# Chunked attention and two mixture-of-experts layers on one core: another order for the attention's loads

## The chip, the cores and the metric

The kernel runs on one core of a Trainium2 chip. A core has TensorE (PE, matrix multiplication; PEld is its weight load), VectorE (DVE), ScalarE (ACT), GpSimd (POOL) and SyncE (SP), each with an instruction stream of its own that is worked off in order, and 16 DMA engines that move data for all of them. Nearly every transfer of this kernel is issued by SP; GpSimd issues the gathers, the scatters and a few copies.

The metric is the device time of one execution in microseconds (us). A profiled execution gives a trace with the start and length of every instruction. Rows of the trace count from the start of its span.

## The reference

Attention runs over `q`, `k`, `v` of shape (2, 8, 768, 64): two batches, eight heads, 768 positions, head size 64. Its output, 1536 rows of 512 numbers, goes through a layer of eight experts with the two best per row, and that layer's output through a second layer of eight experts with one per row and a capacity of 384.

```python
for c in range(768 // 32):                       # chunks of 32 queries
    q_c   = q[:, :, 32*c:32*c+32]
    k_ctx = k[:, :, max(0, 32*c-16):min(768, 32*c+40)]
    k_full = concat([mem_k, k_ctx]);  v_full = concat([mem_v, v_ctx])
    s = (q_c @ k_full.T) / 8
    a = exp(s - max(s));  a = a / (sum(a) + 1e-9)
    out[:, :, 32*c:32*c+32] = a @ v_full
x = out as (1536, 512)
x = sum over each row's two best experts of gate * (relu(x @ w1[e]) @ w2[e])
y = gate * (relu(x @ v1[e]) @ v2[e])             # one expert, if a place is free
```

Every chunk sees the eight memory rows `mem_k`, `mem_v` beside its own context.

## The kernel before

**Attention.** The 1536 rows are 12 tiles of 128, numbered t = 0 to 11; 0 to 5 belong to the first batch, 6 to 11 to the second. A loop runs `step(t)` for t = -2 to 11 as a pipeline: step t makes the scores of tile t + 2 (L240) and their maxima and differences (L253, L256), the transposed probabilities of tile t + 1 (L267, L269), attends with the values of tile t (L281), turns tile t - 1 for its gate logits (L306, L309) and makes those of tile t - 2 (L316), and at its end divides tile t by its sums (`normalise`, L290 to L297). Keys and queries come into SBUF as raw blocks (L120, six per batch, 512 KB each) and are turned on TensorE (`t_unit`, L207) into `kt` and `qz`. The first batch's are turned ahead of the loop. The second batch's turns are 13 units (one of them the memory keys, L197) in a list, from which each step takes as many as the tuple `UP` says: the first half ahead of the probabilities, the second half behind the attending.

Values are loaded per tile and per batch in two shifted copies (L128, 24 loads, rows of 256 bytes). The memory rows are written over certain partitions of each copy from a small tile (`v_mem`, L136), so a `v_mem` waits for its loads, and `L281` for the `v_mem`. The first batch's `v_mem` is issued by POOL, the second's by SP.

**What sets the order.** The schedule is written out by hand: each engine works its instructions in the order of the program. The dictionary `ahead` lists what is issued ahead of which step; -3 stands for ahead of the loop. SP therefore issues all loads of the attention first, and the result of tile t, `put_x(t)` (L300, 256 KB to `x_rows` in memory), can be issued only when SP has come to it, at the start of step t + 1. The result tiles `xs` have four buffers, so `normalise(t)` may write only when `put_x(t - 4)` has landed. The accumulators `psC` of L281 hold one tile, so `attend(t + 1)` waits for `normalise(t)`.

**Behind the attention.** From step 7 on `half_step`, called twice in a step, also splits the first experts' weights (`raww`, L726) into a high and a low part, `whi` on ACT (L743) and `wlo` on DVE (L744); `SPS` says how many at each call. The list of expert jobs follows: V0 and V8 for the first layer's expert 0, S[0] to S[6] for the rest, then U0, UL and R[0] to R[6] for the second layer. Hooks attach other work to the units of a job: eight zero fills of the second layer's input rows (`blank_rows`, L1237, 520 KB each) hang on V0 and V8. A job's `pool` names those of every four splits of the next weights whose low part GpSimd makes instead of DVE.

Of the kernel before, what the change touches and what calls it, by code (L numbers as in the profile page):

```python
# [25 lines left out]
AT = {2: ('lg',), 4: ('w',), 5: ('gw',), 18: ('w',), 24: ('rank',), 27: ('list',), 29: ('w',), 30: ('w',), 32: ('end',)}  # L26
NS = 0
QUICK = 0.7
UP = (0, 3, 3, 3, 3, 1)
WPR = 1  # L30
UU = [0, 0, 0.5, 1, 1, 1.5, 1.5, 1.5, 2, 2, 3, 3]
UWE = 3
# [6 lines left out]
CP = 0.8  # L39
CPP = 2.4  # L40
AH = (0.5, 0.0)
SPS = [2, 0, 3, 0, 1, 1, 2, 1, 2]
RB = 6
ZB = 2
ZT = 5
# [9 lines left out]
def attention_two_moe_kernel(  # L55
# [7 lines left out]
    nc = tc.nc  # L63
# [5 lines left out]
    G = S // 128  # L69
# [19 lines left out]
    def pool(name, side="left", **kw):  # L89
        st_ = ExitStack()  # L90
        pools[name] = st_
        return st_.enter_context(tc.tile_pool(name=name, bufs=1, side=side, **kw))
# [31 lines left out]
    def load_v(b, g, y):  # L124

        r = 128 * g + 32 * y - 16
        p0, p1 = max(0, -r), min(128, S - r)
        nc.sync.dma_start(vw[b][y][p0:p1, g, :, 0:D],  # L128
                          bass.AP(tensor=v.tensor, offset=v.offset + (b * H * S + r + p0) * D,
                                  ap=[[D, p1 - p0], [S * D, H], [1, D]]))  # L130

    def v_mem(b, g0, g1, eng):

        for y in range(2):
            for x in range(2):
                eng.dma_start(vw[b][y][64 * x + 56:64 * x + 64, g0:g1].rearrange("p g h d -> p g (h d)"),  # L136
                              memv[:, b].rearrange("p h d -> p (h d)")[:, None].to_broadcast([NM, g1 - g0, H * (D + 1)]))
# [161 lines left out]
    def put_x(t):  # L299
        nc.sync.dma_start(x_d[NP + 128 * t:NP + 128 * t + 128, 0:DM], xs(t))  # L300
# [22 lines left out]
    def step(t, units):  # L323

        on = 0 <= t < NT
        end = t == NT - 1
        n = UP[t + 2] if t + 2 < len(UP) else 0

        def some(m):
            for _ in range(m):  # L330
                if units:
                    units.pop(0)()

        if t + 2 < NT:
            scores(t + 2)
            submax(t + 2)
        half_step()
        if end:
            flush()
            low = x_block(V0.xg[0], 0, V0.C, "B", True)  # L340
        some((n + 1) // 2)
        pe_part()
        if 0 <= t + 1 < NT:
            prob(t + 1)
        if on:
            attend(t)
        some(n // 2)
        if 0 <= t - 1:
            x_tr(t - 1)
        if 0 <= t - 2:  # L350
            logits(t - 2)
        pe_part()
        if end:
            put = logits(NT - 2, True)
            normalise(t)
            low()
            V0.weight(0)
            put()
        elif on:
            half_step()  # L360
            normalise(t)
# [3 lines left out]
    def y_consts():  # L365

        for i in range(2):
            nc.vector.tensor_copy(yid[:, :, i, 0:128], ident[:, None, :].to_broadcast([128, KD, 128]))
            nc.vector.tensor_copy(yid[:, :, i, 128:136], wg2)
        nc.vector.tensor_tensor(yid[:, :, 0, 136:144], wg2, yid[:, :, 0, 128:136], op=OP.subtract)  # L370
        nc.vector.tensor_copy(yid[:, :, 1, 136:144], zero[:, 0:32].rearrange("p (k e) -> p k e", k=KD))
# [861 lines left out]
    raw_q = [(n, j) for n in range(4) for j in range(2)]  # L1233
    split_q, sps = [], list(SPS)

    def blank_rows(z, n, w):
        nc.sync.dma_start(z, zero[:, None, 0:w].to_broadcast([128, n, w]))  # L1237

    def raw_w0():
        n, j = raw_q.pop(0)  # L1240
        half(n, j, w1a, w2a, 0, n)
# [22 lines left out]
    V0 = Job("T", 0, caps1[0], True, cols=0)  # L1264
    V8 = Job("W", 0, caps1[E], True, cols=E)
# [14 lines left out]
    raw1 = []  # L1280
# [25 lines left out]
    def gates2():  # L1306
# [2 lines left out]
        nc.gpsimd.tensor_copy(noi[:, :, E:V], noi[:, :, 0:1])  # L1309

    lv = lambda b, g: [lambda y=y: load_v(b, g, y) for y in range(2)]
    ahead = {-3: [*lv(0, 0), *lv(0, 1), gates, *sum((lv(0, g) for g in range(2, G)), []), *raw1,
                  *[lambda g=g: v_mem(0, g, g + 1, nc.gpsimd) for g in range(2)],
                  *[lambda g=g: v_mem(0, g, g + 2, nc.gpsimd) for g in (2, 4)],
                  gates2, *sum((lv(1, g) for g in range(G)), [])],
             0: [lambda: v_mem(1, 0, 1, nc.sync), lambda: v_mem(1, 1, G, nc.sync)]}
    for f in ahead.pop(-3):
        f()
    zr = x2_d.rearrange("(t p) c -> p t c", p=128)
# [1 line left out]
    zeros = [(zr[:, ZN * i:ZN * i + ZN], ZN, W2) for i in range((N + NP) // (128 * ZN))]  # L1321
    zeros2 = [(zo[:, 4 * i:4 * i + 4], 4, DM) for i in range(N // 512)]
    for t in range(-2, NT):
        if 0 <= t - 1:
            put_x(t - 1)
        for f in ahead.pop(t, ()):
            f()
        if t == ZT:
            blank_rows(x_d[0:NP].rearrange("(t p) c -> p t c", p=128), 4, W1)
        if t == G:  # L1330
            assert not units and not ahead
            pools["a0p"].close()
            wp["A"] = pool("wpA")
            st["x"] = (wp["A"].tile([128, KD, CM], F32R, name="xh"), wp["A"].tile([128, KD, CM], F32R, name="xl"))
            wp["Z"] = pool("wpZ")
            for _ in range(ZB + RWB):
                raw_w0()
            y_consts()
        if t == G + 1:
            split_q = [(n, c) for n in range(3) for c in range(4)]  # L1340
        step(t, units)
        for i, (t0, t1) in enumerate(BT):
            if t - 2 == t1 - 1 and i < len(BT) - 1:
                routes[i] = route(i)
                state["gen"].append(routes[i])
# [19 lines left out]
    UL = Job("T", n2, caps2[E], False, gate=U0.gate)  # L1365
    R = [Job(kind2(caps2[1 + s]), n2 + 4 + 4 * i, caps2[1 + s], False, gate=U0.gate) for i, s in enumerate(ORDER2)]
# [262 lines left out]
    def hook(job, u, f):  # L1629
        hooks.setdefault((at[job], u), []).append(f)  # L1630

    for j, job in enumerate(jobs[:-1]):
        if jobs[j + 1] in S[1:] + R[1:]:
            early_ = job in R and job.kind == "T" and jobs[j - 1].kind == "M"
            hook(*(jobs[j - 1], FU) if early_ else (job, 0), jobs[j + 1].fetch)
    for j in range(len(zeros)):
        hook(*((V0, j) if j < 3 else (V8, j - 2)), lambda j=j: blank_rows(*zeros[(j + 2) % len(zeros)]))
    for j in range(3):
        hook(S[j], 4, lambda j=j: blank_rows(*zeros2[j]))
        hook(V8, 7, lambda: run_until(lambda: S[0].xg))  # L1640
# [10 lines left out]
    U0.late = drain  # L1651
    U0.weigh = UWE
    U0.pool = (1, 3)
    R[1].pool = (2,)
    UL.pool = (2,)
    S[0].quiet = S[-1].quiet = U0.quiet = 0
    U0.turns = [2 * U0.nb + 6]
    S[-1].turns = [11, 12, 13]
# [69 lines left out]
```

## Time and profile before

| what | value |
|---|---|
| median of 3 runs | 662.37 us (662.33 to 664.4) |
| the profiled execution | 663.03 us |
| its span, first to last instruction | 661.2 us |
| PE busy | 600.5 us (91%) |
| PEld busy | 546.3 us (83%) |
| DVE busy | 385.3 us (58%) |
| ACT busy | 310.9 us (47%) |
| POOL busy | 147.8 us (22%) |
| mean granted TensorE clock | 0.946 |
| DMA traffic | 115.14 MB, 174 GB/s on average |

The profiled execution is 0.66 us above the median, and 1.83 us of it lie outside the span. Idle time of an engine counts only where the engine that sets the end waits for it. A granted clock of 1.00 is TensorE's 2.4 GHz, 0.50 its 1.2 GHz.

### The profile page before, as it was taken

What the parts mean: (1) busy time and instruction counts of PE and PEld (TensorE: products, weight loads), DVE (VectorE), ACT (ScalarE), POOL (GpSimd) and SP (SyncE); (2) the same over time, 40 slices, a digit from 0 to 9 for tenths busy, and PEclk for the clock granted to TensorE, in tenths of its full rate; (3) what the DMA queues carried; (4) which work ended last, traced back from release to release, by engine and by line L of the source; (5) the groups of instructions that cost most, each with busy time, mean ns of one, the idle gap of its engine ahead of it and who ended that gap; (6) DMA issues with size and microseconds to landing.
All of it is one profiled execution on the core that took longest, in us unless ns stands there. A gap on an engine that the chain in (4) does not pass through costs nothing. (4 is left out here: it accounts for less than half of the span.)

```text
span 661.2 us, 12269 instructions
## 1 busy us (share of the span) xinstructions
PE 600.5 (91%) x4514; PEld 546.3 (83%) x4520; DVE 385.3 (58%) x1009; ACT 310.9 (47%) x653; POOL 147.8 (22%) x201
## 2 busy tenths in 40 slices
PE   7197878979999999999999899999999999999991
PEld 5186767769999999999999798988978888888971
DVE  7273484668655555555555337373657647787550
ACT  5063344323544544545445435344336566686551
POOL 7500000013041311312212120202453124120110
PEclk9589685879999999999999989999999999999996
DMA  9996726327895574855636654545366577786540
GB/s 254 234 219 125 258 77 212 95 60 229 300 259 150 143 225 148 210 165 127 170 109 142 176 116 138 124 115 144 37 227 222 168 248 246 253 273 224 191 136 18
DMA packets 89099, 115.14 MB, mean 174 GB/s; under 512 B 40353, under 2 KB 40353, under 8 KB 89032
## 3 DMA queue, kind: packets, MB, share of 16 engines
q1 hardware_dynamic: 79992, 92.00, 45.7%
q0 software_dynamic: 9040, 22.28, 15.2%
q8 instruction: 38, 0.62, 0.4%
q14 instruction: 29, 0.24, 0.1%
HBM read 91.91 MB, written 22.34 MB: 173 GB/s over the span
## 5 line engine op out<-in xcount | busy, mean ns | idle before, releaser
L744 DVE TENSOR_TENSOR wlo<-raww,whi 128x512 fp32r<-128x512 f32 x248 | 170.1, 709 | 40.6 <-ACT whi L743 39.3
L743 ACT ACTIVATE whi<-raww 128x512 fp32r<-128x512 f32 x256 | 152.2, 624 | 13.0 <-DMA raww<-in_moe_w_dram 9.5
L821 DVE SCALAR_TENSOR_TENSOR hl<-psA,hh 128x384 fp32r<-128x384 f32 (+6 forms) x104 | 53.9, 519 | 84.9 <-ACT hh L820 79.8
L820 ACT ACTIVATE hh<-psA 128x384 fp32r<-128x384 f32 (+6 forms) x104 | 47.7, 458 | 115.8 <-PE psA L809 101.5
L809 PE MATMUL psA<-xh,wlo 128*128 128x256 f32 (+6 forms) x416 | 86.6, 331 | 6.0 <-PEq L1096 3.5
L809 PE MATMUL psA<-xl,whi 128*128 128x256 f32 (+6 forms) x416 | 84.0, 325 | 0.0
L809 PE MATMUL psA<-xh,whi 128*128 128x256 f32 (+6 forms) x416 | 83.8, 323 | 0.0
L809 PEld LDWEIGHTS psA<-xh,wlo 128*128 128x128 f32 x416 | 68.2, 191 | 8.0 <-issue 4.2
L809 PEld LDWEIGHTS psA<-xl,whi 128*128 128x128 f32 x416 | 70.0, 191 | 0.4
L809 PEld LDWEIGHTS psA<-xh,whi 128*128 128x128 f32 x416 | 69.4, 189 | 0.3
L893 POOL DMA_INDIRECT x_rows<-yr,ids x25 | 39.1, 1565 | 129.9 <-ACT whi L743 86.4
L749 POOL DMA_INDIRECT xg<-x_rows,ids x37 | 37.7, 1019 | 94.4 <-DVE gs L929 41.1
L809 PE MATMUL psC<-wlo,hh 128*128 128x512 f32 x200 | 57.7, 408 | 0.0
L809 PE MATMUL psC<-whi,hh 128*128 128x512 f32 x200 | 55.6, 396 | 0.0
L809 PE MATMUL psC<-whi,hl 128*128 128x512 f32 x200 | 55.0, 395 | 0.0
L761 DVE TENSOR_TENSOR xl<-psB,xh 128x512 fp32r<-128x512 f32 (+4 forms) x37 | 23.9, 645 | 43.2 <-ACT xh L760 43.2
L809 PEld LDWEIGHTS psC<-whi,hh 128*128 128x128 f32 x200 | 37.4, 189 | 8.5
L809 PEld LDWEIGHTS psC<-whi,hl 128*128 128x128 f32 x200 | 37.5, 188 | 8.3
L760 ACT ACTIVATE xh<-psB 128x512 fp32r<-128x512 f32 (+4 forms) x37 | 20.7, 560 | 44.1 <-PE psB L757 41.9
L809 PEld LDWEIGHTS psC<-wlo,hh 128*128 128x128 f32 x200 | 35.4, 189 | 5.7
L809 PE MATMUL psA<-hh,wlo 128*128 128x312 f32 (+4 forms) x160 | 36.6, 350 | 0.0
L871 ACT ACTIVATE yr<-psC,gs 128x512 f32<-128x512 f32 x25 | 17.2, 687 | 39.0 <-PE psC L809 36.4
(326 smaller groups left out, 899.9 us busy)
## 6 DMA issues: line engine op xcount, KB each, us to landing
raww<-in_moe_w_dram SPq DMA_DIRECT2D x128, 512.0 KB
v<-in_v_dram SPq DMA_DIRECT2D x20, 256.0 KB
x_rows<-zero SPq DMA_DIRECT2D x8, 520.0 KB
raw<-in_k_dram SPq DMA_DIRECT2D x6, 512.0 KB
raw<-in_q_dram SPq DMA_DIRECT2D x6, 512.0 KB
x_rows<-xs SPq DMA_DIRECT2D x12, 256.0 KB
out_dram<-zero SPq DMA_DIRECT2D x3, 1024.0 KB
x_rows<-zero SPq DMA_DIRECT2D x1, 1042.0 KB
```

The lines of the kernel that those rows point to most:

```text
L743: nc.scalar.activation(hi[:, c], raw, AF.Copy)
L744: (eng or nc.vector).tensor_tensor(lo[:, c], raw, hi[:, c], op=OP.subtract)
L749: return nc.gpsimd.indirect_dma_start(out=xg, out_offset=None, in_=src, in_offset=bass.IndirectOffsetOnAxis(ap=ids_ap, axis=0))
L760: nc.scalar.activation(xh[:, :, o], pv[:, :, 0:n], AF.Copy)
L761: low = lambda: nc.vector.tensor_tensor(xl[:, :, o], pv[:, :, 0:n], xh[:, :, o], op=OP.subtract)
L809: nc.tensor.matmul(ps, w[a], x[b], start=first and i == 0, stop=last and i == n - 1)
L820: nc.scalar.activation(hh[:, f, 0:C], ps[:, 0:C], AF.Relu)
L821: nc.vector.scalar_tensor_tensor(hl[:, f, 0:C], ps[:, 0:C], 0.0, hh[:, f, 0:C], op0=OP.max, op1=OP.subtract)
L871: nc.scalar.activation(yr[:n, 0:DM], ps[:n], AF.Copy, scale=g[:n])
L893: wr = nc.gpsimd.indirect_dma_start(out=x2_d, out_offset=off, in_=yr[:n], in_offset=None, compute_op=OP.add)
```

## The change

Four things change in the program; the arithmetic is the same.

1. The loads of the second batch's raw keys and queries are issued between the first batch's values instead of behind them, and the gate weights one tile earlier. The first batch's memory rows are issued tile by tile on POOL, the last two tiles together. The second batch's last two value tiles and its memory rows are moved to the start of steps -1, 1 and 2: SP comes to `put_x(0)` between them, ahead of five of the six tiles' memory rows.
2. `UP` lets the second batch's turns begin in step 0 instead of step -1; `SPS` spreads the same 12 splits over the same nine calls in another way.
3. Three of the eight zero fills are issued at the start of steps 8, 9 and 10 instead of in V0.
4. The jobs UL and R[1] no longer give one split of each four to GpSimd.

```diff
-UP = (0, 3, 3, 3, 3, 1)
+UP = (0, 0, 3, 3, 4, 3)
-SPS = [2, 0, 3, 0, 1, 1, 2, 1, 2]
+SPS = [1, 1, 2, 1, 2, 1, 2, 1, 1]
...
-    ahead = {-3: [*lv(0, 0), *lv(0, 1), gates, *sum((lv(0, g) for g in range(2, G)), []), *raw1,
-                  *[lambda g=g: v_mem(0, g, g + 1, nc.gpsimd) for g in range(2)],
-                  *[lambda g=g: v_mem(0, g, g + 2, nc.gpsimd) for g in (2, 4)],
-                  gates2, *sum((lv(1, g) for g in range(G)), [])],
-             0: [lambda: v_mem(1, 0, 1, nc.sync), lambda: v_mem(1, 1, G, nc.sync)]}
+    mem = lambda b, g0, g1, e: [lambda: v_mem(b, g0, g1, e)]
+    ahead = {-3: [*lv(0, 0), gates, *lv(0, 1), *raw1[0:2], *mem(0, 0, 1, nc.gpsimd), *raw1[2:4], *lv(0, 2),
+                  *mem(0, 1, 2, nc.gpsimd), *raw1[4:6], *lv(0, 3), *mem(0, 2, 3, nc.gpsimd), *lv(0, 4),
+                  *mem(0, 3, 4, nc.gpsimd), *lv(0, 5), *mem(0, 4, 6, nc.gpsimd), gates2,
+                  *lv(1, 0), *lv(1, 1), *lv(1, 2), *lv(1, 3)],
+             -1: [*mem(1, 0, 1, nc.sync), *lv(1, 4), *lv(1, 5)],
+             1: [*mem(1, 1, 3, nc.sync)],
+             2: [*mem(1, 3, 6, nc.sync)]}
...
+        if 8 <= t < 11:
+            blank_rows(*zeros[t - 6])
...
-    for j in range(len(zeros)):
-        hook(*((V0, j) if j < 3 else (V8, j - 2)), lambda j=j: blank_rows(*zeros[(j + 2) % len(zeros)]))
+    for j in range(3, len(zeros)):
+        hook(V8, j - 2, lambda j=j: blank_rows(*zeros[(j + 2) % len(zeros)]))
...
-    R[1].pool = (2,)
-    UL.pool = (2,)
```

On SP, where the last values of the second batch (`v10`, `v11`) are loaded, the kernel before has the rest in this order: the memory rows of all tiles, then the results.

```order
L128 DMA v11_78<-in_v_dram 112x8x64
L136 DMA v10_77<-memv_84 8x520 x2
L136 DMA v11_78<-memv_84 8x520 x2
L136 DMA v10_77<-memv_84 8x5x520 x2
L136 DMA v11_78<-memv_84 8x5x520 x2
L300 DMA x_rows<-xs_491 128x512
L300 DMA x_rows<-xs_594 128x512
```

At the same place on SP the changed kernel has tile 6's memory rows ahead of the last two tiles' loads, and then this order; `xs_470` is the result of tile 0.

```order
L128 DMA v11_78<-in_v_dram 112x8x64
L300 DMA x_rows<-xs_470 128x512
L136 DMA v10_77<-memv_84 8x2x520 x2
L136 DMA v11_78<-memv_84 8x2x520 x2
L300 DMA x_rows<-xs_577 128x512
L136 DMA v10_77<-memv_84 8x3x520 x2
L136 DMA v11_78<-memv_84 8x3x520 x2
L300 DMA x_rows<-xs_697 128x512
```

The first result now follows the last value load at once, and memory rows stand between the first three results.

On PE, at the end of the turns ahead of the loop, the kernel before has the second batch's first turn (`raw_279`) ahead of the probabilities of tile 0 (`sm_340`).

```order
L240 MATMUL psA_346<-kt0_79,qz0_81 64x64 x16
L197 MATMUL psD_369<-ident_104,memk_83 64x32 x2
L207 MATMUL psD_373<-ident_104,raw_279 128x128 x4
L267 MATMUL psB_380<-ident_104,sm_340 128x128 x4
L207 MATMUL psB_387<-ident_104,raw_281 128x128 x4
L240 MATMUL psA_402<-kt0_79,qz0_81 64x64 x16
```

There the changed kernel has the probabilities of tile 0 and the scores of tile 2 first; the first raw block is now `raw_271`.

```order
L240 MATMUL psA_354<-kt0_79,qz0_81 64x64 x16
L267 MATMUL psB_377<-ident_104,sm_340 128x128 x4
L240 MATMUL psA_384<-kt0_79,qz0_81 64x64 x16
L197 MATMUL psD_407<-ident_104,memk_83 64x32 x2
L207 MATMUL psD_411<-ident_104,raw_271 128x128 x4
L267 MATMUL psB_418<-ident_104,sm_371 128x128 x4
L281 MATMUL psC_425<-v00_75,ex_382 32x65
```

The first turn moved behind one probability and one score group; the attending of tile 0 follows it closely.

## Rows read from the trace of the kernel before

**Rows 1.** Waits, 0 to 150 us: engine, line, for whom; sum us, times, longest.

```profile
PE psD L207 <- DMA raw<-in_k_dram: 13.2, 1, 13.2
PE psB L757 <- DMA xg<-x_rows,ids_l: 3.2, 2, 1.9
```

**Rows 2.** Stretches: us; busy (instructions) of PE, PEld, DVE, ACT, POOL; clock, DMA share, GB/s.

```profile
40.00:58.00 18.00, 16.77 (x381) 14.55 (x375) 13.54 (x41) 11.94 (x30) 0.24 (x2) 1.00 0.89 177
60.00:64.00 4.00, 2.24 (x42) 1.99 (x42) 0.52 (x4) 0.45 (x1) 0.00 (x0) 1.00 0.45 50
68.70:76.50 7.80, 7.47 (x115) 6.85 (x116) 4.23 (x18) 2.20 (x7) 0.00 (x0) 0.50 0.59 212
100.60:106.70 6.10, 5.01 (x85) 4.37 (x86) 3.23 (x11) 3.23 (x8) 0.00 (x0) 0.57 0.60 179
106.70:120.00 13.30, 12.58 (x104) 11.20 (x105) 4.23 (x14) 5.01 (x14) 0.00 (x0) 0.50 0.62 200
115.00:118.00 3.00, 3.00 (x13) 2.66 (x12) 0.69 (x1) 1.11 (x2) 0.00 (x0) 0.50 0.80 294
140.00:640.00 500.00, 490.76 (x2907) 455.00 (x2908) 300.21 (x735) 252.21 (x518) 117.27 (x136) 0.99 0.61 178
```

**Rows 3.** Timeline, attention up to tile 4: start, us, engine, line, what, [idle before, releaser].

```profile
4.60 1.09 PE L207 MATMUL psB<-ident,raw 128*128 128x128 f32 x4 [0.22 <-DMA raw<-in_k_dram]
30.93 1.11 PE L207 MATMUL psD<-ident,raw 128*128 128x128 f32 x4 [13.19 <-DMA raw<-in_k_dram]
...
60.95 0.20 DVE L292 RECIPROCAL rs<-rs 128x8 f32<-128x8 f32 x1
67.98 0.42 DVE L295 TENSOR_TENSOR xs<-psC,rs 128x256 f32<-128x256 f32 x1 [6.83 <-DMA x_rows<-xs]
68.66 2.02 PE L281 MATMUL psC<-v,ex 64*32 64x65 f32 x64 [6.26 <-DVE xs L295]
73.88 0.42 DVE L295 TENSOR_TENSOR xs<-psC,rs 128x256 f32<-128x256 f32 x1
```

**Rows 4.** Timeline of SP, 0 to 200 us: issue start, us, what.

```profile
0.76 0.46 SPq L120 DMA_DIRECT2D raw<-in_k_dram  x1
37.79 17.04 SPq L128 DMA_DIRECT2D v<-in_v_dram  x12
54.93 6.92 SPq L136 DMA_DIRECT2D v<-memv  x8
61.97 7.27 SPq L300 DMA_DIRECT2D x_rows<-xs  x5
94.08 0.43 SPq L300 DMA_DIRECT2D x_rows<-xs  x1
97.20 0.38 SPq L726 DMA_DIRECT2D raww<-in_moe_w_dram  x1
128.27 1.08 SPq L1237 DMA_DIRECT2D x_rows<-zero  x2
```

**Rows 5.** Timeline of steps 9 and 10.

```profile
100.39 1.41 ACT L743 ACTIVATE whi<-raww 128x512 fp32r<-128x512 f32 x2
100.56 1.24 PE L281 MATMUL psC<-v,ex 64*32 64x65 f32 x64 [2.35 <-ACT xs L297]
```

**Rows 6.** All instructions of the weight split's low part: ns shortest/median/longest, first and last start.

```profile
L744 DVE TENSOR_TENSOR wlo<-raww,whi x248: 671/690/2282, 83.1 to 638.0; 128x512 fp32r<-128x512 f32 x124
L744 POOL TENSOR_TENSOR wlo<-raww,whi x8: 1276/1291/1760, 467.3 to 551.9; 128x512 fp32r<-128x512 f32 x8
```

**Rows 7.** Waits, 488 to 512 us, and timeline around 552 us.

```profile
PE psA L809 <- DVE hl L821: 0.4, 1, 0.4
...
551.65 2.11 DVE L744 TENSOR_TENSOR wlo<-raww,whi 128x512 fp32r<-128x512 f32 x1 [0.62 <-ACT whi L743]
551.91 1.29 POOL L744 TENSOR_TENSOR wlo<-raww,whi 128x512 fp32r<-128x512 f32 x1
554.15 0.74 PE L809 MATMUL psA<-xh,wlo 128*128 128x256 f32 x4 [1.44 <-DVE hl L821]
```

## The prediction

> **What bounds the kernel now.** I first read the stretches, to see who sets the end. From 140 to 640 us TensorE is busy for 490.76 of 500 us at a granted clock of 0.99 [rows 2]: from there the expert jobs run at TensorE's pace, and whatever the attention ends earlier the whole kernel ends earlier. So the question is what sets the attention's pace. The waits up to 150 us name TensorE's longest: 13.2 us for the second batch's first raw keys [rows 1], from about 17.7 to 30.93 us [rows 3]. It is tempting to book these 13.2 us as the gain. But the timeline shows a later wait: the sums of tile 4 are inverted at 60.95 + 0.20 = 61.15 us, its product starts at 67.98, released by the transfer of a result, and TensorE, whose accumulators hold one tile, starts to attend tile 5 at 68.66 after 6.26 us of idling [rows 3]. This is `normalise(4)` waiting for the buffer of `put_x(0)`. A wait behind another one takes over what the first gives back, so what counts is when `put_x(0)` lands, not when the keys come. SP's rows say why it lands so late: SP issues the second batch's values from 37.79 to 54.83, its memory rows from 54.93 to 61.85, and only at 61.97 the first result, which was long computed [rows 4].
>
> **The new order of the loads.** Step by step:
>
> (a) *The keys' wait.* Twelve value loads take 17.04 us, 1.42 each [rows 4]. Eight fewer stand ahead of the first raw keys: they land at 30.93 - 8 x 1.42 = 19.6 us instead. From that turn to the waiting `normalise(4)` the kernel before took 61.15 - 30.93 = 30.2 us [rows 3]; the same work, now begun with step 0, gets there at about 50. The values and raw blocks ahead of the second batch's values are the same set in both orders, so this set is still issued by 37.79; tile 5's values come last in it, then four copies of memory rows on POOL, so steps 4 and 5 have theirs by about 45. Call it 46 to 52 us. All of this is earlier than `put_x(0)`, so it buys nothing by itself; it makes room.
>
> (b) *The first result.* Its place on SP is now behind the last value load, and four of the eight memory-row issues still precede it. The values' issue ended at 54.83; four issues cost 6.92 / 2 = 3.5 us of SP's time if nothing hides them and nothing if they are issued while SP waits for room in its queue anyway, as it does while 1.42 us pass per value load. I take the middle, issue at 54.83 + 1.75 = 56.6. For the landing I take the first raw block, which went through an empty queue: issued at 0.76 [rows 4], its turn starts at 4.60 [rows 3], 3.8 us. So `put_x(0)` lands at 60.4 us, 7.6 us ahead of 67.98. Bounds: 54.83 + 3.8 = 58.6, a gain of 9.4; and 54.83 + 3.5 + 6.0 (the loaded queue's 61.97 to 67.98) = 64.3, a gain of 3.7. TensorE then idles from about 50 to 60.4, once, where it idled twice.
>
> (c) *After the wait* TensorE starts at 1.2 GHz again, as it did before: granted clock 0.50 from 68.7 to 76.5, after an idle stretch of 6.26 us [rows 2, 3]. The longer idling costs no more on this account, since the half clock is paid after the restart. So steps 5 to 11 move up as a block.
>
> **The splits' order.** Twelve splits of 0.69 us on DVE [rows 6] stay twelve; at any of the calls at most one or two more or fewer stand ahead of a `normalise`. Where ACT had three in a row it has two. That is up to 1.4 us either way in one step, returned in another: 0, with 1.4 on either side.
>
> **The zero fills.** Three fills of 520 KB leave V0's stretch, at 294 GB/s [rows 2] 1.8 us each. One of them was issued at 128.27 with a second one [rows 4], just ahead of the gathers for which TensorE waits 3.2 us in all [rows 1]. At most 1.8 us of that go; most of it is the gathers' own time, so I take 0.3. Their cost at the new place is hidden if DMA is idle there; if not, it is the last rival below.
>
> **The second layer's splits.** Eight low parts run on GpSimd, 1.29 us each; six of them (UL, R[1]) go to DVE at 0.69 [rows 6]. The third of R[1] overlaps a DVE split which takes 2.11 us instead of 0.69, and TensorE waits 1.44 us for the `hl` behind it [rows 7]. Afterwards DVE does two in 1.38, 0.7 earlier. The same place in UL costs 0.4 us [rows 7], which goes. Together -1.1; the bounds are -1.84 (both gaps gone) and +4.1 (six more DVE splits, all on the path; DVE is busy 300 of 500 us there [rows 2], so mostly they are not). The Trainium skill (SBUF — State Buffer, Who interferes with whom) says that a DVE instruction with two SBUF inputs contends with a GpSimd instruction that reads SBUF, and that the one that comes second is blocked for the whole instruction. The 2.11 us row agrees. By that rule alone DVE would get back up to 6 x 1.29 us and pay 6 x 0.69, 3.6 us; TensorE would still see only its two gaps.
>
> **Sum.** -7.6 + 0 - 0.3 - 1.1 = -9.0 us against the profiled execution's 663.03, so 654.0; that execution lies 0.66 above the median, which gives 653.4.
>
> **Rivals.**
>
> *Memory rows between the results.* Tiles 7 and 8 now have their memory rows between `put_x(0)` and `put_x(1)`, tiles 9 to 11 theirs before `put_x(2)`. The 60 to 64 us row, when almost only memory rows moved, shows 50 GB/s [rows 2]. 64 rows of 2080 bytes are then 2.7 us, 96 are 4.0, and `put_x(2)` lands at about 60.4 + 6.7 + 1 = 68. `normalise(6)` comes two steps of 5.9 us (67.98 to 73.88, [rows 3]) after 60.4, at 72. So it is hidden by 4 us. If `put_x(2)` comes 8 us later than that, the wait costs about 4 us: 657.4. The Trainium skill (DMA: Bandwidth & Descriptors, Rules for kernel authors) has a rule that speaks for this rival: an outermost dimension under 16 confines a transfer to that many DMA engines, here eight partitions to eight, so that a result behind it is complete only when these eight are through. The DMA share of 0.45 in that row agrees.
>
> *The clock comes back earlier.* From 100.6 to 120 us TensorE works 5.01 + 12.58 us at 0.57 and 0.50 [rows 2], after gaps such as the 2.35 us ahead of tile 10 [rows 5]. If the more even splits take such a gap away, up to half of these 17.6 us can come back; I take 5: 648.4. For it: ACT's three splits in a row. Against: DVE's work is unchanged, and other gaps can start it.
>
> *Hidden anyway.* The loads' bytes are the same and they move at 0.89 of the engines' time up to 58 us [rows 2]. If the new mixture runs less well, the last values come later, and `put_x(0)` lands when it did; only the small terms remain: 662.37 - 1.4 = 661.0. Against: 6.92 us of memory-row issues demonstrably stood between the values and the result.
>
> *Slower: the fills ahead of the weights.* In steps 8 to 10 a 520 KB fill goes into SP's queue ahead of the weight half that the next step splits. ACT works in order: a split that waits for its half holds the exponentials and the products behind it. Price: 3 x 1.8 = 5.3 us, and if TensorE then stays at 1.2 GHz in these steps, half of about 5.65 us of work per step (7.47 us in 7.8, scaled to 5.9, [rows 2, 3]), 8.5 in all: +13.8, so 667.2. It decides if the halves land after their split is called; for it speaks that ACT's two splits at 100.39 take 1.41 us, a half issued at 97.20 arriving at the last moment [rows 4, 5]. Against: the fill follows the result issued at 94.08, 3.1 us before the half [rows 4], and is through in 1.8.
>
> **Chances and range.** Forecast 0.55, memory rows 0.12, clock 0.15, hidden 0.07, slower 0.08, anything else, mostly a smaller gain, 0.03. About 0.3%, 2.0 us, can be told from no change. Forecast, memory rows, clock and the rest are faster: 0.85. Hidden is within 0.3%: 0.07. Slower: 0.08. The forecast's own terms give 663.03 - 0.66 - (3.7 to 9.4), shifted by 1.4 either way and by the tail; with the clock's case below and the memory rows above the range is 646.5 to 660.0.
>
> **What would show it.** In the profile after: TensorE's 13.2 us wait gone and one longer idle stretch up to about 60 us, released by `x_rows<-xs`; SP's first result issued near 56 to 57 us; no wait for a result in steps 5 and 6; the granted clock back at 1.00 some 8 us after the restart; V0 starting 7 to 8 us earlier; no 2 us DVE split in UL and R[1]. It is wrong if `normalise(4)` starts after 64 us, if a second wait for results follows, or if ACT waits for `raww` in steps 9 to 11.

## The result and the profile after

The changed kernel takes 651.95 us (median of 4 runs, 650.34 to 652.55); on the same chip the kernel before takes 662.35 (4 runs, 660.64 to 664.4). The ratio is 0.984 with a 95% interval of 0.981 to 0.987: faster by 10.4 us, where 9.0 were forecast. The profiled execution has a span of 650.8 us at a mean clock of 0.952; before it was 661.2 at 0.946.

First the attention up to tile 7, from the timeline of the changed kernel (start, us, engine, line, what, [idle before, releaser]); it answers to [rows 3].

```profile
20.98 0.66 PE L207 MATMUL psD<-ident,raw 128*128 128x128 f32 x4
...
60.29 0.42 DVE L295 TENSOR_TENSOR xs<-psC,rs 128x256 f32<-128x256 f32 x1 [9.87 <-DMA x_rows<-xs]
60.97 1.26 PE L281 MATMUL psC<-v,ex 64*32 64x65 f32 x36 [9.30 <-DVE xs L295]
...
77.05 0.63 ACT L743 ACTIVATE whi<-raww 128x512 fp32r<-128x512 f32 x1 [3.61 <-DMA raww<-in_moe_w_dram]
...
80.62 0.42 DVE L295 TENSOR_TENSOR xs<-psC,rs 128x256 f32<-128x256 f32 x1
81.19 1.41 PE L281 MATMUL psC<-v,ex 64*32 64x65 f32 x64 [2.21 <-DVE xs L295]
```

The second batch's first raw keys are used at 20.98 without a wait of their own; the 13.2 us are gone. TensorE idles once for a result, 9.30 us up to 60.97, and `normalise(4)` starts at 60.29 instead of 67.98. At 77.05 there is a wait that the profile of the kernel before did not have: ACT's first weight split waits 3.61 us for `raww`. `normalise(7)`, which releases TensorE's tile 8, comes behind it. The same split and the two `normalise` around it in the kernel before:

```profile
80.10 0.42 DVE L295 TENSOR_TENSOR xs<-psC,rs 128x256 f32<-128x256 f32 x1
81.71 1.15 ACT L743 ACTIVATE whi<-raww 128x512 fp32r<-128x512 f32 x2 [0.29 <-issue]
86.03 0.42 DVE L295 TENSOR_TENSOR xs<-psC,rs 128x256 f32<-128x256 f32 x1
```

Now SP's timeline after, which answers to [rows 4]: issue start, us, what.

```profile
39.48 10.27 SPq L128 DMA_DIRECT2D v<-in_v_dram  x8
49.85 2.86 SPq L136 DMA_DIRECT2D v<-memv  x4
52.75 2.92 SPq L128 DMA_DIRECT2D v<-in_v_dram  x4
55.78 1.10 SPq L300 DMA_DIRECT2D x_rows<-xs  x1
...
66.56 0.38 SPq L1237 DMA_DIRECT2D x_rows<-zero  x1
67.14 0.37 SPq L300 DMA_DIRECT2D x_rows<-xs  x1
67.87 3.95 SPq L726 DMA_DIRECT2D raww<-in_moe_w_dram  x4
```

The first result is issued at 55.78, and the first weight halves at 67.87, right behind the 1042 KB fill of the routing rows.

Last the waits of 0 to 150 us (engine, line, for whom; sum us, times, longest), against [rows 1], and one row of the stretches (columns as in [rows 2]).

```profile
PE psC L281 <- DVE xs L295: 12.2, 3, 9.3
PE psB L757 <- DMA xg<-x_rows,ids_l: 3.4, 2, 2.1
ACT whi L743 <- DMA raww<-in_moe_w_dram: 4.9, 3, 3.6
```

```profile
140.00:640.00 500.00, 492.07 (x2912) 454.76 (x2910) 299.47 (x743) 255.29 (x524) 110.28 (x133) 1.00 0.62 180
```

TensorE is as full in the expert jobs as before, so what the front gains reaches the end. Where the 10.9 us between the last matmuls of the two profiles came from, by TensorE's timeline:

| stretch | before | after | difference |
|---|---|---|---|
| start to V0's first matmul | 114.01 | 108.52 | -5.49 |
| from there to the last matmul ahead of the branch L1096 | 263.93 | 264.99 | +1.06 |
| from there, past the branch, to the first routing matmul of layer two (441.08, 432.49) | 63.14 | 58.98 | -4.16 |
| to the first transpose of the gathered rows (485.62, 477.28) | 44.54 | 44.79 | +0.25 |
| to the last matmul of the jobs | 161.92 | 159.35 | -2.57 |

The forecast had no term at all for the third row. In it lies a branch behind the first layer's last stage, with a gap of 3.48 us in the one profile and 0.85 in the other.

### The profile page after: what moved, and what is told of

Its sections match the earlier page's. It is cut to its first block, busy times and chain, and to the rows that moved or that the text cites. A ratio compares the mean times of both kernels' runs of the same rounds, so it can differ in the third digit from the quotient of the medians.

```text
span 650.8 us, 12271 instructions
## 1 busy us (share of the span) xinstructions
PE 600.4 (92%) x4520; PEld 544.6 (84%) x4520; DVE 384.1 (59%) x1015; ACT 311.2 (48%) x653; POOL 141.1 (22%) x199
## 5 line engine op out<-in xcount | busy, mean ns | idle before, releaser
L896 POOL DMA_INDIRECT out_dram<-yr,oids x13 | 13.1, 1008 | 111.5 <-ACT yr L871 84.9
```

Source lines behind the costliest of these rows:

```text
L896: wr = nc.gpsimd.indirect_dma_start(out=out, out_offset=off, in_=yr[:n, 0:DM], in_offset=None, bounds_check=N - 1, oob_is_err=False)
```

## The experiments

My theory: TensorE's restart is set by the landing of the first result, and the keys only make room. Rivals: the keys' 13.2 us are themselves the gain; the fills or the splits matter more than I booked; the loads as a whole bound the front. The edits are to the changed kernel unless said otherwise.

**Results first, keys late** (the kernel before, with only this changed).

```
-3: the list ends with lv(1, 0) to lv(1, 3)
-1: mem(1, 0, 1), lv(1, 4), lv(1, 5);  1: mem(1, 1, 3);  2: mem(1, 3, 6)
```

> The kernel before with one part of the change alone: the second batch's last two value tiles and its memory rows at the starts of steps -1, 1 and 2, so that SP comes to the first result right behind the last value load. The raw keys still come behind all of the first batch's values. My theory (the landing of put_x(0) sets the attention's pace): TensorE still waits some 13 us for the keys, but normalise(4) starts at about 61 us, when its sums are ready, instead of 67.98, and TensorE's idle stretch of 6.26 us before tile 5 goes; V0 starts 4 to 7 us earlier and the time is 4 to 7 us under the kernel before. Rival (the keys' earlier arrival makes the gain): the 13 us wait stays, so the time stays within 1.5 us of the kernel before.

Measured 652.39 us, ratio 0.987 (0.980 to 0.995). Its timeline:

```profile
31.70 1.12 PE L207 MATMUL psD<-ident,raw 128*128 128x128 f32 x4 [13.76 <-DMA raw<-in_k_dram]
...
60.79 0.42 DVE L295 TENSOR_TENSOR xs<-psC,rs 128x256 f32<-128x256 f32 x1
```

The whole wait for the keys is still there, and `normalise(4)` starts at 60.79 all the same, now without a wait for a result. V0 starts at 106.59. The last run below is the changed kernel with the split numbers that this one has, so up to V0 the two differ by the place of the keys and queries among the first batch's loads, by the turns and by the fills; V0 starts at 106.90 there. The gain came without the keys, and the keys added nothing to it.

**Keys first, results late.**

```
-3: ... lv(1, 0) to lv(1, 5);  0: mem(1, 0, 1), mem(1, 1, G);  nothing at -1, 1, 2
```

> The changed kernel with the second batch's values and memory rows ahead of the first result again, as the kernel before has them; keys and queries still between the values, turns from step 0. My theory: the 13 us wait for keys is gone, yet normalise(4) starts at 66 to 68 us as before, TensorE's idle stretch ahead of it grows to 14 to 17 us, and of the 10.4 us only 2 to 5 stay (the second layer's splits and the branch behind S[4]). Rival (the keys make the gain): normalise(4) at about 60 us and the time within 1.5 us of the changed kernel.

Measured 654.9 us, ratio 0.993 (0.990 to 0.997). Its timeline:

```profile
68.30 0.42 DVE L295 TENSOR_TENSOR xs<-psC,rs 128x256 f32<-128x256 f32 x1 [18.08 <-DMA x_rows<-xs]
68.98 2.02 PE L281 MATMUL psC<-v,ex 64*32 64x65 f32 x64 [17.51 <-DVE xs L295]
```

The 13.2 us did not go away; they joined the next wait, 17.51 us in one piece, and V0 starts at 112.52, 1.5 us earlier than before. That this kernel still beats the one before is mostly its tail (the last row of the table, -2.55 us) and the row with the branch (-4.27 us).

**GpSimd's splits back.** `R[1].pool = (2,)` and `UL.pool = (2,)` restored.

> The changed kernel with one split of four on GpSimd again in UL and R[1]. My theory: TensorE's gaps of 0.4 us and 1.4 us at the ends of these two jobs return, DVE splits of over 2 us too, and the time is 1.1 to 2.5 us above the changed kernel's. Rival (DVE is not on the path there): within 0.5 us of it. The branch behind S[4], where TensorE idled 3.48 us in the profile of the kernel before and 0.85 us in that of the changed kernel: if the change caused the difference it is 0.85 us here; if it varies from run to run it can be either here and in the other three.

Measured 649.59 us, ratio 0.985 (0.979 to 0.991). All instructions of the low part (ns shortest, median, longest), and TensorE's waits from 480 to 600 us:

```profile
L744 DVE TENSOR_TENSOR wlo<-raww,whi x248: 671/690/2281, 74.9 to 624.2; 128x512 fp32r<-128x512 f32 x124
L744 POOL TENSOR_TENSOR wlo<-raww,whi x8: 1282/1292/1757, 452.1 to 538.6; 128x512 fp32r<-128x512 f32 x8
```

```profile
PE psA L809 <- DVE hl L821: 1.8, 2, 1.5
```

The 2.28 us DVE split is back, and both gaps with it. From the first transpose of the gathered rows to the last matmul it takes 161.39 us, against 159.35 in the changed kernel: this is worth 2.0 us in that stretch. In the four profiles of programs with GpSimd's splits in these jobs the stretch takes 161.39 to 163.38 us, in the ten without them 159.00 to 160.58. The time did not show it: 1.1 to 2.5 us more were expected, and it is not above the changed kernel's. In the profile, V0 started 2.5 us earlier (106.05) and the stretch from there to the branch was 3.6 us shorter, 261.41 us. The half clock ahead of V0 ended 3.1 us behind V0's start there and 8.5 in the changed kernel; no run shows that the edit caused this.

**Routing fill behind the weights.** `ZT = 7` instead of 5.

> The changed kernel with the 1042 KB zero fill of x_rows at the start of step 7 instead of step 5, behind the first four weight halves on SP's queue instead of ahead of them. In the changed kernel's profile ACT waits 3.6 us in step 7 for the first half (raww), and TensorE idles 1.2 and 2.2 us there. My theory (the weights stand behind the fill in the queue): the first half lands about 3.5 us earlier, that wait goes, normalise(7) starts 2 to 3.5 us earlier, and the time is 2 to 3.5 us under the changed kernel's. Rival (the results and memory rows ahead of it delay it, or steps 8 to 10 have the next wait): under 0.7 us.

Measured 647.55 us, ratio 0.979 (0.973 to 0.985). The first split starts at 72.59 instead of 77.05, `normalise(7)` at 76.16 instead of 80.62, and V0 at 106.12 instead of 108.52: of 4.5 us half is left at V0 (against the second profile of the changed kernel, below, 2.9 and 1.7). From the issue of the first weight half to its split it takes 5.20 us here, and 9.18 and 7.83 in the two profiles of the changed kernel. So the fill that stands ahead of the weights makes most of the wait of step 7, which gave back part of the forecast; 1.59 us of it stay, since ACT comes to the split earlier.

**Results between the values.**

```
-3: ... lv(1, 0);  1: lv(1, 1), mem(1, 0, 1), lv(1, 2);  2: lv(1, 3), mem(1, 1, 3), lv(1, 4)
3: lv(1, 5), mem(1, 3, 5);  4: mem(1, 5, 6)
```

> The changed kernel, with the second batch's values drawn apart further: only its first tile's values stand ahead of the steps, the others and the memory rows follow one or two at a time behind the first, second, third and fourth results. Theory: what sets the restart of normalise(4) is the landing of the first result and nothing else. It is then issued near 42 us instead of 55.8 and lands near 46; normalise(4) starts when its sums are ready, 47 to 53 us, and the idle stretch of TensorE from 51.7 to 61.0 goes. The next wait is already known: ACT's first split waits for raww, which cannot be issued before tile 5 is attended, and the blank fill of the routing rows is ahead of it; so of the 9.3 us some 4 to 6 reach the end: 645 to 649, ratio against before near 0.977. Rival one, the loads as a whole bound the steps (the keys, values and results of the second batch share one stream that has no room): the values then come late for tiles 6 to 8, the idle time reappears there, and the time is that of the changed kernel, 651 to 653. Rival two, the results between the values hold the second batch's loads back so far that it is slower than the changed kernel, over 654.

Measured 650.57 us, ratio 0.985 (0.980 to 0.990), against 650.86 for the changed kernel on that chip. ACT's and TensorE's timeline:

```profile
75.76 0.63 ACT L743 ACTIVATE whi<-raww 128x512 fp32r<-128x512 f32 x1 [12.90 <-DMA raww<-in_moe_w_dram]
```

```profile
79.89 2.15 PE L281 MATMUL psC<-v,ex 64*32 64x65 f32 x64 [13.05 <-DVE xs L295]
```

My theory was right on the result and wrong on what it is worth. `normalise(4)` runs at 52.36, 8 us earlier, and nothing is gained: TensorE now idles 13.05 us at tile 8. From the first result to the first weights SP pauses for less than 0.8 us between any two issues, and it comes to them at 69.11 (67.87 in the changed kernel). As long as the first split waits for these weights, the order of what stands ahead of them doesn't matter. Rival one held.

**The same, and the fill in step 7.** `ZT = 7` beside the edit before.

> The kernel of the run before (results between the second batch's values) and the blank fill of the routing rows in step 7 instead of 5, behind the first halves of weights instead of ahead of them. Theory: both waits of the changed kernel go, the one for the first result and ACT's for the first raww in step 7; each alone uncovers the other, so together they bring more than the first alone: 640 to 645, V0 starting at 99 to 103 us. Rival, the fill's place is only moved to a later step (as the norm times of the run with the fill alone moved suggest, 83.7 and 91.6 us for tiles 8 and 9): 645 to 649, the same as without the move.

Measured 648.61 us, ratio 0.982 (0.977 to 0.987). The split starts at 72.30 and TensorE still idles 11.38 us ahead of tile 8 (the tile called 7 in the expectations: the `normalise` behind the split is that of tile 7, the tile that TensorE then attends is 8). V0 starts at 104.63, where I expected 99 to 103. It is the rival's number, not mine.

**Zero fills back** in V0's stretch.

```
-        if 8 <= t < 11:
-            blank_rows(*zeros[t - 6])
+    for j in range(len(zeros)): hook(*((V0, j) if j < 3 else (V8, j - 2)), ...)
```

> The changed kernel with its three zero fills taken out of steps 8 to 10 and put back into V0's stretch, where the kernel before had them. Theory: at the one place and at the other they are hidden but for a few tenths of a microsecond; V0 starts within 0.7 us of 108.5, and the time stays within 1.5 us of the changed kernel's. Rival (the slower case of the prediction): in steps 8 to 10 they hold the weight halves back and ACT's splits wait for raww; then V0 starts 1.5 to 5 us earlier without them, the waits for raww after 80 us go, and the time is 647 to 650. Second rival: beside V0 they hold the gathers back; then the waits for ids_l in V8 grow by over 1 us, and it is slower.

Measured 649.95 us, ratio 0.983 (0.978 to 0.988). V0 starts at 107.92 (107.79 in the run of the changed kernel beside it), and TensorE's waits for `ids_l` are 2.8 us against 2.7. ACT's waits for `raww` behind step 7 are 0.40 and 1.26 us without the fills there. So the fills cost nothing that can be seen at either place.

**The changed kernel again.**

> The changed kernel as it is, once more, on the chip of the three others. Theory: the gap of TensorE at the branch behind the last stage of the first layer (3.5 us in the profile of before, 0.9 after) is not the change's: here it can be anything from 0.3 to 3.5 us, while all starts up to V0 repeat within 0.5 us (normalise(4) at 60.3, normalise(7) at 80.6, V0 at 108.5) and the gaps in the second layer's splits stay away. Rival: it is the change's, and the gap is again under 1 us with no half clock behind it. The median is between 650 and 653 by the first; by the second the same.

Measured 650.86 us, ratio 0.986 (0.981 to 0.991). `normalise(4)` starts at 60.08, `normalise(7)` at 79.02 and V0 at 107.79; the gap at the branch is 0.50. I expected the starts to repeat within 0.5 us. They differ by up to 1.6, so a difference of a microsecond between two single profiles shows little.

**No split in step 7.** The run with the results between the values and `ZT = 7`, with

```
-SPS = [1, 1, 2, 1, 2, 1, 2, 1, 1]
+SPS = [0, 0, 1, 2, 2, 2, 2, 2, 1]
```

> The kernel with the results between the second batch's values and the blank fill in step 7, and in addition no weight split in step 7: the numbers of splits per half step are 0, 0, 1, 2, 2, 2, 2, 2, 1. Theory: in the run without this edit TensorE idled 11.4 us ahead of tile 7 because normalise(6) stood behind ACT's first split, which waited from 61 to 72.3 us for raww; the first weights land at 72 in any order of the loads, since everything that SP issues ahead of them is the same. With the split behind normalise(6) and normalise(7) this idle stretch is spread out or gone: normalise(7) at 64 to 67 us instead of 75.9, normalise(8) at 70 to 76. What follows is then TensorE's and DVE's own pace with 12 splits in three steps; V0 starts at 96 to 101 instead of 104.6, and the time is 640 to 646. Rival: V0 cannot start before its twelve splits, whose weights come at one per 3 us from 72 on, so that V0 starts at 104 again and the time stays within 1.5 us of 648.6.

Measured 645.31 us, ratio 0.977 (0.974 to 0.980): the best of all, some 6 us below the changed kernel. TensorE's timeline:

```profile
64.63 1.40 PE L281 MATMUL psC<-v,ex 64*32 64x65 f32 x64 [0.49 <-DVE xs L295]
73.40 0.20 PE L525 MATMUL psD<-msk,tri 128*128 128x45 bf16 x1 [5.98 <-DVE lgs L317]
84.45 1.96 PE L281 MATMUL psC<-v,ex 64*32 64x65 f32 x64 [3.77 <-ACT xs L297]
95.68 2.09 PE L281 MATMUL psC<-v,ex 64*32 64x65 f32 x64 [4.18 <-issue]
```

`normalise(7)` starts at 64.06 instead of 75.86. But 10 of these 12 us are given back: the routing's sums (L525) and the last tiles now wait behind splits that wait for weights, and V0 starts at 102.92, 1.7 us earlier. My 96 to 101 was too good; the time is inside my range.

**The first split one call later, in the changed kernel.** `SPS = [0, 1, 2, 1, 2, 2, 2, 1, 1]`.

> The changed kernel with 0, 1, 2, 1, 2, 2, 2, 1, 1 splits per half step instead of 1, 1, 2, 1, 2, 1, 2, 1, 1: the first split one call later, behind normalise(6). Theory: the wait of 3.6 us of ACT for raww in step 7, which the prediction did not foresee, gave back 2 to 2.6 us of the gain at tile 4. Without it normalise(7) starts at 77.5 to 78.5 us instead of 79 to 80.6, and if nothing else takes it V0 at 105.5 to 107; time 648 to 650. Rival: the wait is only moved by one call, since raww lands at 75 to 77 anyway; then normalise(8) starts at 86 to 88 as it did and the time is 650 to 652.

Measured 649.92 us, ratio 0.984 (0.980 to 0.987). ACT's timeline:

```profile
75.17 0.63 ACT L743 ACTIVATE whi<-raww 128x512 fp32r<-128x512 f32 x1 [0.50 <-DMA raww<-in_moe_w_dram]
```

The wait for the first weights shrinks to 0.50 us, `normalise(7)` starts at 77.67 and `normalise(8)` at 84.73, both 1.4 to 3.0 us earlier than in the two profiles of the changed kernel. That is the theory's side; the rival had 86 to 88 for tile 8. But V0 starts at 107.18, only 0.6 us ahead of the nearer of these two profiles, which differ by 0.7 themselves, and the times can't tell the two kernels apart. What takes the rest back between tile 8 and V0 was not tried.

**The kernel before again.**

> The kernel before as it is, profiled once more. Theory: the gap of TensorE at the branch behind the last stage of the first layer (3.48 us and half clock after it in the first profile of this kernel) is not bound to the kernel: here it is under 1 us or absent in the same place, as in seven of the nine other profiles, and the last matmul of the main part ends 2 to 5 us earlier than the 647.5 us of the first profile; V0 starts at 114.0 within 0.7. Rival: it is bound to the program, and the gap is again 2.9 to 3.5 us.

One run, 661.81 us. The gap at the branch is 2.16 us and the last matmul ends at 646.22, so the theory's "under 1 us" was wrong; V0 starts at 113.03. Between the two second profiles the same table reads -5.24, +0.89, -1.65, -0.90 and -4.02, in sum -10.92: what V0 gains repeats, the places behind it vary.

**Numbers of splits of before.** `SPS = [2, 0, 3, 0, 1, 1, 2, 1, 2]`.

> The changed kernel with the numbers of weight splits per half step that the kernel before had (2, 0, 3, 0, 1, 1, 2, 1, 2 instead of 1, 1, 2, 1, 2, 1, 2, 1, 1), all else as changed. Theory (the prediction's term for the order of the splits, 0 with 1.4 on either side): normalise(7) up to 0.7 us later than 79.0 to 80.6, two splits instead of one standing ahead of it behind the same raww, and V0 within 1.4 us of 107.8 to 108.5; time 650 to 652.5. Rival: with the first result early the order matters more than I said, since the second split of step 7 waits for a half that lands 1.5 us after the first; V0 1.5 to 3 us later, time 652.5 to 655. Beside it: the gap of TensorE at the branch behind the last stage of the first layer was 3.48, 2.16 and 2.89 us in the three profiles of programs with these numbers, and 0.9 at most in the nine with the new numbers. If it goes with the numbers of splits it is over 2 us here; if it goes with something else that those three share, it is under 1 us.

Measured 651.67 us, ratio 0.988 (0.985 to 0.992). V0 starts at 106.90, 0.9 to 1.6 us earlier than with the new numbers, and the gap at the branch is back: 3.20 us. The stretch from V0 to the branch takes 261.90 us, 3.1 less than in the two profiles of the changed kernel, and takes back most of what the row with the branch loses: the clock was at 0.50 from 99.83 to 110.08 here, and from 96.56 to 117.04 and 92.43 to 116.32 there. Whether the numbers or chance decide that, no run separates. (The new numbers and the two other edits of them stood in ten profiles, not nine; the gap was 0.85 at most in all ten.) So the gap goes with `SPS`, 260 us behind the steps where it acts. The branch's own row (ns, start) and TensorE's row behind it in the timeline, first of the kernel before, then of the changed one:

```profile
L1096 PEldq COMPARE_BRANCH  x1: 4857/4857/4857, 376.3 to 376.3; - x1
```

```profile
381.42 1.62 PE L809 MATMUL psA<-xh,wlo 128*128 128x384 f32 x4 [3.48 <-PEq L1096]
```

```profile
L1096 PEldq COMPARE_BRANCH  x1: 2307/2307/2307, 371.9 to 371.9; - x1
```

```profile
374.36 0.94 PE L809 MATMUL psA<-xh,wlo 128*128 128x384 f32 x4 [0.85 <-PEq L1096]
```

The branch is the same instruction and takes 2.3 us in one and 4.9 in the other. The DMA view has a queue for instructions, and around the branch it moves one packet of 16 KB (the rows do not say for which engine). Read from the trace (us):

| kernel | PE's own semaphore instructions ahead | branch reached | packet from, to | branch done |
|---|---|---|---|---|
| before | 66 | 376.33 | 377.99, 379.68 | 381.19 |
| before's split numbers | 69 | 366.89 | 369.10, 370.32 | 371.83 |
| after | 71 | 371.88 | 371.72, 372.68 | 374.19 |
| after again | 71 | 370.90 | 370.66, 371.64 | 373.15 |

In each of these the branch ends 1.5 us after the packet is through (1.36 to 1.53 us in all fourteen profiles). That is what one would see if TensorE's sequencer waited for code; no run delayed the packet by itself. In the four profiles with the old numbers the packet starts 0.9 to 2.2 us after the branch is reached, in the ten others from 0.9 before to 0.2 after. The instructions ahead are 66 to 69 in the four and 70 to 73 in the ten, so where the program's blocks are cut would explain it; that was not tried by itself and stays open. The Trainium skill (Runtime: NRT & Kernel Launch, Instruction fetch mechanics) says that instructions come in 16 KiB blocks through the sequencer's own DMA queue, and that a taken branch to a target outside the loaded blocks waits for a fetch. The packet's size and the branch's end behind it agree; no row here shows where the target lay.

## Why the prediction was right, and where by luck

The mechanism was right and is shown: the run with the results alone has the gain, the run with the keys alone has not. The size came out near the forecast by luck: what the forecast had too much in one place it lacked in two others, and one of these it had not looked at.

(a) and (b): forecast issue 56.6 and landing 60.4; measured 55.78, and `normalise(4)` at 60.29 (60.08 in the second profile). The term of -7.6 measured -7.7 there, and -6.6 between the second profiles.

(c), "steps 5 to 11 move up as a block", is the step that failed. Tile 6 is 8.0 us earlier, tile 7 only 5.4, and V0 5.5 (5.2 between the second profiles). I looked for a later wait on results and on the fills, not on the first weights: SP issues them behind everything, at 67.87, and the routing fill lies just ahead of them. ACT waits 3.61 us for them in step 7, and of the 7.7 us only 5.5 reach V0. The half clock after the restart was foreseen: it ends at 69.25, 8.3 us behind it. But it is not the same every time, which (c) took for granted. Between the second profiles tile 4 is 6.6 us earlier, tile 6 only 4.6 and tile 7 4.1: the kernel before was then at half clock for 3.4 us (67.17 to 70.59), the changed one for 10.2 (58.30 to 68.53), and the kernel before also waited 1.96 us for its first weights. So that the block came apart is seen in both pairs; that the weights take the most of it is seen in the first pair and in the run with the fill behind them.

The splits' order, 0 with 1.4 on either side, was wrong in place and size: with the new numbers V0 starts 0.9 to 1.6 us later (by single profiles, and at a different clock), but the gap at the branch is 2.6 us shorter, and in the profile of before 3.4 us at half clock followed it (381.36 to 384.77), which is another 1.7. These 4.2 us of the first profiles' difference (1.7 between the second ones) were not in my view, since I had put down all from 140 us on to TensorE's pace. Between the times the edit makes no difference that they can tell (651.67 and 650.86).

The zero fills, -0.3: none. The gathers' wait is 3.4 against 3.2 in [rows 1], and moving the fills back changes nothing.

The second layer's splits, -1.1, were too small: -2.6 between the profiles, -2.0 by the run that puts them back. All three gaps went, 0.40, 1.44 and one of 0.50 that I had not listed, and the 0.7 us that I expected to pay for two splits in a row did not come. The longest split on DVE fell from 2282 ns [rows 6] to 695. The Trainium skill (SBUF — State Buffer, Who interferes with whom) says that a DVE instruction with two SBUF inputs contends with a GpSimd instruction that reads SBUF; the run that puts GpSimd's splits back, with its 2281 ns, agrees. The order that the prediction took from there, that the second to come is blocked, does not fit this row: the DVE split of 2.11 us in [rows 7] started 0.26 us ahead of GpSimd's, which took its usual 1.29 us.

The rivals: *memory rows between the results* did not appear, no wait for a result follows the first. *The clock earlier* did not happen in the changed kernel: 96.56 to 117.04 is at 0.50, as long as before (101.46 to 121.94). It can happen: in the run with GpSimd's splits back and in the one with the old split numbers this stretch lasted only 10.2 us, and from V0 to the branch they took 261.4 and 261.9 us, against 263.2 to 265.3 in the other profiles. *Hidden anyway* is refuted by the run with the results first. *Slower, the fills ahead of the weights*: ACT does wait for `raww` in steps 9 to 11, 0.37 and 0.95 us, which the prediction had named as a sign of being wrong; but the fills are not the reason, since 0.40 and 1.26 us stay with the fills moved back. The one fill that does hold weights back was there before, in step 5; SP then issued the first half only at 75.53, and ACT waited for no transfer at that split (1.96 us in the second profile).

So 9.0 against 10.4 is a sum of one term that was right at its place, 2.2 us too much behind it, 1.5 too little at the tail, and some 4 us at a branch that I did not see. Without the branch's row the first profiles would differ by 6.8 us.

## What to carry to other kernels

When a wait is moved, ask what the same queue still has to issue for the next stage: here SP came to the first weights at 66 to 69 us in every version that issues the first result early, and moving results within its stream moved the idle time, from tile 5 to tile 8, without shortening it. To gain, take the consumer that waits for the last of the stream (the first weight split) out of the way of the others, as the best version does. And compare two profiles stretch by stretch to the end, also where nothing was changed: here 1.7 to 4.2 of 10.9 us sat behind a branch.

## What the runs showed of the hardware

A conditional branch on TensorE took 1.5 to 4.9 us from being reached to being done, and ended 1.36 to 1.53 us after a 16 KB packet on the instruction queue was through, while on SP, ACT, DVE and GpSimd the same branch took 0.05 to 0.07 us. A DVE split that started 0.26 to 0.43 us ahead of one on GpSimd took 2.11 to 2.28 us instead of 0.69, and GpSimd's took 1.29 to 1.31. With no wait in the way and the clock at 1.00, a step of the attention takes 4.27 us (65.06 to 69.34 between two `normalise` in the run with the results first); the 5.9 us that I took from the profile of before was a step that ran at half clock.
